# Half of an input projection by seven-product block multiplication for six of seven feature chunks, and a head without the early spatial-weight transpose

## The chip, the cores and the metric

One core of a Trainium2 chip. The metric is the device time of one execution in microseconds (us), a median over runs. A profiled span is about 1.7 us shorter than the time of the run that it was taken from (231.8 and 233.52 for the kernel before), so spans are compared with spans and timed runs with timed runs.

In the views of the profile PE is the tensor engine and PEld its weight loads, DVE is the vector engine, ACT the scalar engine, POOL the Pool engine, and SPq the queue that issues most transfers. A row of a timeline has the start and length in us, then engine, line of the kernel, operation, what it writes<-reads, its shape, how many in a row, and in brackets the idle time before it with what ended it. PSUM ("psum") is the memory that products are summed in; a bank here is a piece of it of 128x512 fp32.

## The reference

Two blocks with residuals on a sequence of 2048 tokens of width 512, in bf16: linear attention with 32 heads, then a gated MLP whose gate mixes tokens through a 2048x2048 spatial weight.

```python
h  = x + A(layernorm(x), wqkv, wo)              # linear attention
def B(x, w_in, w_sp, b_sp, w_out):              # on layernorm(h)
    z  = gelu(x @ w_in)                         # 2048 x 1792, F/2 = 896
    z1 = z[..., :896]                           # first half: the change is here
    z2 = layernorm(z[..., 896:])
    g  = einsum('ts,bsf->btf', w_sp, z2) + b_sp
    return (z1 * g) @ w_out
h2 = h + B(layernorm(h), ...)
```

## The kernel before

The program is a list of operations with data dependences; a fixed order string says in what order each engine takes its own, and semaphore waits follow from the dependences. So moving an operation within an engine's order is an edit of that string. The parts that the change touches:

```python
def matmuls(out_ap, pairs, start=True, stop=True, onto=False):   # L402: one matmul per pair
    ...
# first half of the input projection, transposed: 7 feature chunks x 4 token groups of 512
Z1B = [6, 7]
k = 0
for tg in range(NG):
    for fc in range(KF):
        b = Z1B[k % 2]
        k += 1
        matmuls(bank(b), [(win1[:, c, fc * P:(fc + 1) * P], hnT[:, c, tg * GW:(tg + 1) * GW]) for c in range(KD)])
        act(z1T[:, fc, tg * GW:(tg + 1) * GW], bank(b), ACT.Gelu_apprx_tanh, GW).soft.add(table.i)
# (cut) the spatial weight comes by transposing DMA, 16 row tiles; the first EARLY = 1 of them whole and in the head
for i, t in enumerate(order):
    w = NT // 2 if EARLY <= i < NT // 2 else NT
    for j in range(0, NT, w):
        op = dma_t(wsp[:, j:j + w, t * P:(t + 1) * P], B_w_sp[t * P:(t + 1) * P, j * P:(j + w) * P], ...)
        ...
        if i < EARLY:
            first_xt.soft.add(op.i)     # the head's own transposes queue behind it
```

In the head (the first 20 us) tiles of x are normalised, transposed (six by the tensor engine, ten by DMA), multiplied by the key weight, and summed with their keys. The second half of the projection ("z2") starts at about 65 us, and the spatial product with its own seven-product cells at about 120.

Of the kernel before, what the change touches and what calls it, by code (L numbers as in the profile page):

```python
# [18 lines left out]
class _Op:
# [233 lines left out]
def bass_sequential_preLN__linear_attn_block__mixer_gmlp__prompt_kernel(  # L253
# [130 lines left out]
    def bank(b, n=512, lo=0):  # L384
        return psum[:, b, lo:lo + n]
# [220 lines left out]
    def next_pair():  # L606
        pc[0] += 1
        return PAIRS[pc[0] % 2]

    CB, first_xt, second = [4, 5, 6, 7], None, None  # L610
    HEAD, SINGLE = 6, 4
    ACTS = (1,)
    QSPLIT, KSPLIT, CACT = (6, 7), (), 2


    def k_unit(n):
        nonlocal first_xt, second
        b = next_pair()
        for i in (n, n + 1):
            if i in ACTS:  # L620
                s = st[0][:, i, :]
                act(sh_t[0], x[:, i, :], ACT.Identity, D, accum=s[:, 0:1])
                act(sh_t[1], x[:, i, :], ACT.Square, D, scale=D ** -0.5, accum=s[:, 1:2])
                moments(s, 6, D)
                rpow(s[:, 7:8], rs[0][:, i, 0:1])
            else:
                op = stats(x, 0, i)
                if i == 0:
                    second = warmup(16, 60, op)
                if n == 0:  # L630
                    rstd_act(st[0], rs[0], i, 1, 6)
        if n == 2:
            rstd_act(st[0], rs[0], n, 2, 6)
        elif n:
            rstd(st[0], rs[0], n, 2, 6, n >= HEAD)
        for i in (n, n + 1):
            norm("DVE" if n < HEAD else "ACT", xn[:, i, :], x[:, i, :], st[0], rs[0], i, 6, D)
            if n < HEAD:
                pe_transposes(xn[:, i, :], b + i % 2, xnT, i, second)
            else:  # L640
                g.last = dma_t(xnT[:, :, i * P:(i + 1) * P], xn[:, i, :], f"xt{i}")
                if i == HEAD:
                    first_xt = g.last
        for i in (n, n + 1):
            matmuls(bank(b + i % 2), [(xnT[:, c, i * P:(i + 1) * P], wqkv[:, c, D:2 * D]) for c in range(KD)])
        if n < SINGLE:
            for i in (n, n + 1):
                phi(pk[:, i:i + 1, :], b + i % 2, 1)
        else:
            phi(pk[:, n:n + 2, :], b, 2, n in KSPLIT)  # L650

        def fn(pe, i):
            inst = None
            for c in range(KD):
                inst = pe.matmul(bank(CB[c]), lhsT=xn[:, i, c * P:(c + 1) * P], rhs=pk[:, i, :],  # L655
                                 start=i == 0, stop=i == NT - 1)
# [180 lines left out]
    order = [t for p in range(NG // 2) for tg in (p, p + NG // 2) for t in range(tg * TPG, (tg + 1) * TPG)]
    prev = late
# [181 lines left out]
```

## Time and profile before

| | before |
|---|---|
| median of the timed runs | 233.21 us |
| profiled span | 231.8 us |
| tensor engine with work | 224.6 us, 97% |
| first pair "pk,xn" of tiles 4 and 5 starts | 20.32 us |
| first z2 group starts | 65.01 us |
| last matmul starts | 228.95 us |

The last three rows are marks read off the timeline: the start of one easily recognised instruction at the end of the head, at the start of the second part, and at the end. Because the tensor engine is nearly always full, the difference of a mark between two kernels says in which of three stretches time was won or lost. The page's lines stand in the prediction.

### The profile page before, as it was taken

What the parts mean: (1) busy time and instruction counts of PE and PEld (TensorE: products, weight loads), DVE (VectorE), ACT (ScalarE), POOL (GpSimd) and SP (SyncE); (2) the same over time, 40 slices, a digit from 0 to 9 for tenths busy, and PEclk for the clock granted to TensorE, in tenths of its full rate; (3) what the DMA queues carried; (4) which work ended last, traced back from release to release, by engine and by line L of the source; (5) the groups of instructions that cost most, each with busy time, mean ns of one, the idle gap of its engine ahead of it and who ended that gap; (6) DMA issues with size and microseconds to landing.
All of it is one profiled execution on the core that took longest, in us unless ns stands there. A gap on an engine that the chain in (4) does not pass through costs nothing.

```text
span 231.8 us, 3231 instructions
## 1 busy us (share of the span) xinstructions
PE 224.6 (97%) x1180; PEld 112.1 (48%) x1203; DVE 161.6 (70%) x323; ACT 104.3 (45%) x193; POOL 44.2 (19%) x134
## 2 busy tenths in 40 slices
PE   8997999999999999999999999999999999999995
PEld 8543444453445443454544444444455555555452
DVE  4998755646987550237489989979795566785485
ACT  5694754399989876679862010101021211123010
POOL 3436300000466608023771000000000000000000
PEclk9999999999999999999999999999999999999999
DMA  5893259947546635968999700000000000020025
GB/s 182 263 214 70 59 138 230 315 147 181 114 89 136 117 71 121 183 126 188 185 228 197 159 3 0 0 0 0 3 0 1 0 3 0 20 72 3 0 80 191
DMA packets 58864, 23.68 MB, mean 102 GB/s; under 512 B 48480, under 2 KB 58720, under 8 KB 58848
## 3 DMA queue, kind: packets, MB, share of 16 engines
q1 hardware_dynamic: 58144, 22.88, 44.7%
q10 hardware_dynamic: 704, 0.59, 0.8%
q8 instruction: 9, 0.15, 0.3%
q14 instruction: 7, 0.06, 0.1%
HBM read 7.47 MB, written 2.10 MB: 41 GB/s over the span
## 4 chain that ended last, share of the span: by engine, by line
PE 86%; DMA 6%; ACT 3%; DVE 2%; issue 1%; SPq 0%
PE psum L402 70%; PE psum L802 6%; PE psum L655 5%; PE psum L805 4%; DMA x<-in_A_x_dram 3%; DMA xnT<-xn 2%; DMA hnT<-hn 1%; DVE st L511 1%; ACT sh L421 1%; ACT xn L421 1%; ACT e L421 0%; ACT xnT L421 0%; PE psum L751 0%; PE psum L676 0%; PE psum L720 0%
## 5 line engine op out<-in xcount | busy, mean ns | idle before, releaser
L421 ACT ACTIVATE psum<-psum 128x256 f32<-128x256 f32 (+1 forms) x33 | 14.3, 445 | 90.8 <-PE psum L402 63.1
L402 PE MATMUL psum<-wsp,z 128*128 128x512 bf16 x204 | 47.5, 379 | 0.2
L402 PEld LDWEIGHTS psum<-wsp,z 128*128 128x128 bf16 x208 | 20.4, 98 | 22.9
L402 PE MATMUL psum<-hnT,win 128*128 128x512 bf16 x108 | 25.6, 379 | 0.2
L421 ACT ACTIVATE e<-psum 128x1024 bf16<-128x1024 f32 (+1 forms) x18 | 16.7, 926 | 15.2 <-PE psum L402 14.3
L402 PE MATMUL psum<-t,s 128*128 128x512 bf16 x94 | 22.1, 379 | 0.1
L421 ACT ACTIVATE z1T<-psum 128x512 bf16<-128x512 f32 x28 | 16.6, 594 | 4.9 <-PE psum L402 4.8
L802 PE MATMUL psum<-win,hnT 128*128 128x512 bf16 x64 | 16.4, 379 | 0.4 <-DMA hnT<-hn 0.4
L402 PE MATMUL psum<-wout,z1T 128*128 128x256 bf16 (+1 forms) x82 | 16.6, 314 | 0.1
L402 PEld LDWEIGHTS psum<-hnT,win 128*128 128x128 bf16 x112 | 10.0, 98 | 13.2 <-ACT z1T L421 3.8
L402 PE MATMUL psum<-wqkv,xnT 128*128 128x512 bf16 x61 | 14.8, 380 | 1.4 <-DMA xnT<-xn 1.2
L421 ACT ACTIVATE z<-psum 128x896 bf16<-128x896 f32 x16 | 14.5, 909 | 2.9 <-PE psum L805 2.8
L402 PE MATMUL psum<-xnT,wqkv 128*128 128x512 bf16 x61 | 15.1, 379 | 0.3 <-issue 0.2
L655 PE MATMUL psum<-pk,xn 128*128 128x512 bf16 x64 | 15.3, 379 | 0.0
L402 PE MATMUL psum<-m,pqT 128*128 128x512 bf16 x62 | 14.7, 379 | 0.3 <-DVE h L776 0.2
L776 DVE SCALAR_TENSOR_TENSOR h<-psum,x 128x512 bf16<-128x512 f32 x16 | 10.8, 688 | 5.2 <-PE psum L402 5.1
L402 PEld LDWEIGHTS psum<-t,s 128*128 128x128 bf16 x96 | 9.4, 98 | 10.3
L582 DVE TENSOR_SCALAR e<-e 128x1024 bf16<-128x1024 bf16 (+1 forms) x18 | 7.1, 397 | 9.1 <-ACT e L421 9.0
L805 PE MATMUL psum<-win,hnT 128*128 128x384 bf16 x64 | 13.0, 326 | 0.0
L924 DVE TENSOR_TENSOR u<-psum,bsp 128x512 bf16<-128x512 f32 x16 | 11.0, 687 | 2.8 <-PE psum L402 2.7
L556 DVE TENSOR_SCALAR z<-z,st,rs 128x896 bf16<-128x896 bf16 x16 | 7.2, 493 | 7.3 <-POOL rs L519 7.3
L511 DVE BATCH_NORM_STATS2 st<-x 128x6 f32<-128x512 bf16 x15 | 9.7, 677 | 3.6 <-DMA x<-in_A_x_dram 3.6
(113 smaller groups left out, 349.3 us busy)
## 6 DMA issues: line engine op xcount, KB each, us to landing
r<-rcp SPq DMA_DIRECT2D x16, 128.0 KB, 2.6
out_dram<-h SPq DMA_DIRECT2D x15, 128.0 KB, 1.8
win<-in_B_w_in_dram SPq DMA_DIRECT2D x2, 896.0 KB, 6.6
x<-in_A_x_dram SPq DMA_DIRECT2D x6, 256.0 KB, 4.5
wqkv<-in_A_wqkv_dram SPq DMA_DIRECT2D x2, 512.0 KB, 5.2
wout<-in_B_w_out_dram SPq DMA_DIRECT2D x1, 896.0 KB, 7.2
wo<-in_A_wo_dram SPq DMA_DIRECT2D x1, 512.0 KB, 8.3
bsp<-in_B_b_sp_dram SPq DMA_DIRECT2D x1, 512.0 KB, 5.1
```

The costliest lines, as they stand in the source:

```text
L402: inst = pe.matmul(out_ap, lhsT=a, rhs=b, start=start and i == 0, stop=stop and i == len(pairs) - 1, **kw)
L421: return g.add("ACT", lambda ac: ac.activation(out_ap, in_ap, func, **kw), [in_ap, *extra], [out_ap] + ([accum] if accum is not None else []),
L511: dve(lambda v: v.bn_stats(s[:, 0:6], src[:, n, :]), [src[:, n, :]], [s[:, 0:6]], D)
L556: return dve(lambda v: v.tensor_scalar(dst, src, mean, rst, op0=ALU.subtract, op1=ALU.mult), [src, mean, rst], [dst], w + 460, acc=4)
L582: dve(lambda v: v.tensor_scalar(e, e, 1.0, EPS_PHI, op0=ALU.min, op1=ALU.add), [e], [e], w * GW, acc=4)
L655: inst = pe.matmul(bank(CB[c]), lhsT=xn[:, i, c * P:(c + 1) * P], rhs=pk[:, i, :], start=i == 0, stop=i == NT - 1)
L776: dve(lambda v, n=n, b=b, s=s: v.scalar_tensor_tensor(h[:, n, :], bank(b), 1.0, x[:, n, :], op0=ALU.mult, op1=ALU.add, accum_out=s[:, 0:1] ...
L802: pe.matmul(bank(b), lhsT=hnT[:, c, n * P:(n + 1) * P], rhs=win2[:, c, 0:GW], start=c == 0, stop=c == KD - 1)
L805: inst = pe.matmul(bank(b + 1, F2), lhsT=hnT[:, c, n * P:(n + 1) * P], rhs=win2[:, c, GW:FH], start=c == 0, stop=c == KD - 1)
L924: dve(lambda v: v.tensor_tensor(t, bank(b), add, ALU.add), [bank(b), add], [t], GW, ps=True)
```

## The change

Its intent: with feature chunks k and k + 3, even and odd token tiles, and the 512-long sum split in two, four output blocks make one cell. The ordinary way takes 4 groups x 4 matmuls = 16; seven block products of 2 matmuls take 14, at the price of sums of weights, of inputs and of products. Six cells replace 24 of the 28 groups; the seventh chunk stays ordinary. The sums of inputs and weights lie in columns of the spatial weight's buffer that are loaded later (token groups 1 and 3). The early load of that weight goes too. The head's first loads, statistics and the whole order string are changed with it.

```diff
-EARLY = 1
+EARLY = 0
-ORDER = "c-jTQ17H..."                       (cut)
+ORDER = "c-jrogMt..."                       (cut)
...
+    def strassen(k, q, banks, p5):
+        A, B, C, E = banks
...
+        matmuls(quad(A), list(zip(w11, a11)))
+        copy(bank(B), bank(A))
+        matmuls(quad(E), list(zip(t1, s1)))
+        copy(p5, bank(E))
+        matmuls(quad(A), list(zip(w21, a12)), **onto)
+        gelu(k, q, 0, A)
+        matmuls(quad(B), list(zip(t2, s2)), **onto)
+        dve(lambda v: v.tensor_tensor(bank(C), bank(B), p5, ALU.add), [bank(B), p5], [bank(C)], GW, ps=True)
+        matmuls(quad(B), list(zip(t3, s3)), **onto)
+        matmuls(quad(C), list(zip(w22, s4)), **onto)
+        gelu(k + HF, q, 0, C)
+        dve(lambda v: v.tensor_tensor(bank(E), bank(B), p5, ALU.add), [bank(B), p5], [bank(E)], GW, ps=True)
+        matmuls(quad(B), list(zip(t4, a22)), **onto)
+        gelu(k + HF, q, 1, E)
+        gelu(k, q, 1, B)
...
+    comb(ts[0], w12, w11, ALU.subtract)      # 4 weight sums; the same for 4 input sums in each half
...
+        for k in range(HF):
+            if k not in CLASSIC.get(2 * q, ()):
+                strassen(k, q, ZB[cells % len(ZB)], p5z[cells % 2])
```

Here w and a are blocks of the weights and the inputs, t and s their sums, and A, B, C, E the four PSUM banks of a cell.

More of the change, by code (lines that the diff above doesn't have):

```diff
@@ L13 @@
 GRAN = 16
-EARLY = 1
+EARLY = 0
 SEM_NS = 45.0
-ORDER = "c-jTQ17HvU00h8Cwq47%ZQHhO+qGrewr$(CZ5wwH5gAbt9Wf9Su@D<^5Eu2800D@ED2Rr5$b~$}jl4*LqyUHz2nE3iiC_qhWJrz_NQp#9j8w>n{3w9JNQ(-ngvO|hifD@XNQl%(gMui6bjW~0NROh(gp4SL;;4eE$c!dvhAgOttSEtOsEO>Tj&A6I?kI_#D23)|fpBPrmgt4v=!-tcfm*16wy2FdXpPdSi+UJ`GAN7sXn-*oi}6^7B{+=bSc-PYiE=294rqh+XoyA_fPol{e&~-u=!i}@g3dUILzsYxn1sn#foYh6Ay|pf2#+ubi&cn#)i{b{IDz9BieU)ENCaUNMq>@uVLGOw3%X(^W?%v4<1|iU78YVH*5eGG;uKz@fg0)sp5qy2V-AL61U6tJ7GW`VU^_NpGqzwZ=3x)^VkdTCH_qWK_F+E`U@Nxa3a;WjF5n_A;U+HQ8gAh_Zr~N(;5FXjHtypN?&2OEA~+u)1Vi#2BJdF+G7{h8F`nQjKHvvF;uk*QAHLu-zTqprBPPMH49!ps!&o$9Gb*DoGNUja<1-H9G91J6H)1dqQ!@`UGdlA!3-hx8(=aX5F+DRdBQvoaOS2ZqeEfr~EJ*P$$}kwSF*|cGCkwGWb1{GkSeQjvl*L$=3Au#z*pj)~gSA<lCE13Fn3xr~m}Oa?OIe4l*qXiBmVH=}l~|co*p6$smJQgDjaZfK*^@Qcm`&J=eVLTWS%RgQgvq#t$(4dlnUc-9hbgp-TbWvEG@MgdjoUbaBiWA~*pZ#sp99#L138Gxxt%+>f-5<d={22=)L1pSjx(4+d%2HY*p1EDg4LN)sgzl1704hC<zRMaR}SM4Hc=L(Q$~$qCQai^o?%vHQ+DN0PUTiE<y9W#S3VU`K^0aZ713E9VR02z2^CXml~fs(S1Fa%9UkQ|-sKg(;Z>H?6TW2y&EkF@;6bkE25#hNj^S92<4*44A&%#4&f#3H;yg~^ah~9OF63cO;wEn9J>KU7KIBQB;yb?Q2cF}3Uf@OU=4r0xHD2c>HdQk<R|~aND^2DCPUIq1RAp7tA3o(X{$&+a)fawcHHBAeB~u%<RXep;2X#~@bygR3RRn!waD`A!g;Xtl<a6HOO+MlazT_>w;wS!NL|x`<J|+}NRAhbU5B}sY-e!CyP!xqyXh~rdRbgcXD4~8ckrFG3s;h>gD~3KZreZ0!!YP`PDvshRnBr-G`e?9ftFC6Kj%I3zhN_+hs;_2ixVmYIrfQJ7tG{|^l~!w-rYle*HCMybQzO(*qclz%G+MnBr16@ddFrkC8lzd7sC8PPC0eMpO5(Aaqyw6xrCOuOTBh~dsLfiWE!wJs+NPvltP@(U?b@Xk+N71*p}jh+L)xvK+Nb?GqCGmQ<4Wk0I;GP(qeMQY#LnfjI;RvquM4`QD@y5$itl8;rcb)A54x<Yx}&?grJK5^+`g{|O6>#=@JBt;L#6U#J<|(4(Nm@MXT8=drE_{e*B8CiS7q=!z125;*AFFk7XQ*uW%O_T6a7bjmEXZ^!*XbcabAaX2#0lehjSWda#m+{HWzR~M{q<(avn!@WJh-t7jkw-a|{=DKF4t^$8-+obP*SIF_&>!7k3HQbA88kBR6&vH*hmIbxD_ULr-!GH+OlrbSw9A8~1h}w{}IBb|qK#1o!hq_jP{{a67kkdk^#=5AiTp@nBbVIoEInS95jObS>9*M|bu{*Ku8UcMnhTR8MmUZ}Mgj^(+r}Cy(?DPxlsg@np|*kViPsvpvsqJl6}n$V)um3%%G&J<g-u)nmQfqrA+kywYpD*6SSG!F@yV+|!}F)$jF2x7E#KyxJ=~-s`==+q~U7ywkh<AMVe{ZU"
@@ new lines @@
+ORDER = "c-jrogMttU00qE@tj)G<d$VoZwz=81ZQHhO+jiZ}FHA&4MpVQ_03sm@q9HnBASPlVHsT;Y5+E1yAUE;?AdJumgRlsO;0S?m2#=5uk{}V1A{mk+1yUju5+fh-BNYmu5YnPNDxw0Kpb{D(9uguo(x4y;BONlJ2+|`EnUE1hQ4Cp88C8%OjnNcYP!-uw1KCj=-BAKv(F5I364j6c)zJ*i(Go4t6TQ#}z0n3WQ46h53bj!Obx|5+Fb3mL5A`t?<FO1&upDjC8aYuG<<K7O&>sWP7yZxy4bTvSFc3@85uI=t2XO?4FaZ-W8I!OAE3q0=Fb#vT4na7IV~BuNIDz9Bg5el}kywLK7>%izj?U<U8JLOrSb&o_jagWT^;nBDIE5E@iOG73DVnP1c!t@SgP|CP4cLf9Sd2~Bf$f-!dDx6C*o!^biGA3G-8hG{*otj9kNr4+E4YelxPaukh!jexRJx8ExP+Uyj9Yk%*LZ_hxQ#owi~G2T2MErG2*HqihX{Ox07m3{JjN4*W>|({DE`DJe83NU#AkfLH^kt-|GR(TJHFx%Vlo!PGaP>-G9xi6qi~wyG7e)i9#b(IQ!_L3Fh8>}I`c9O$*eRBFdqvtEz>bQGcY5?zX--mEXA^{$%M?t?99QOEX`a@z;cYwKo(+Q7GY7=VKLTXU6$YyCSqciXBpP!V%B2|wq^xZWF=N+71n11He@3<W^N{7awcVQCS!NDWG}8^8&+ixR%Z(KW;3Q_6Sm?~F5_CZWlwJ5R+eOHZDShs;ZP3a6pr9jj^uRC;Bby&HP&ELHfMTeP&>9~U+!UMrBzn#Wfo;uPMu*oWm5-sWIuLdS7uUwX4G~L;AoEFSPo<^1u?hssWS(09LIA9cXB4DaTaHDIp=UL=kYAh@jTaY0w?hT^XLe3sDJ{MSA~>cg;iWdRZvBAhwHh4CA5(jSxP0<jnmbIGc<$~IiLGjM!UG1`+0yzSxm=xmz7jnl~qnxc$}Mfj|+K_D|mt{d6I*<fQvYpr+A4oHA}NKM{|`-^E6)zv`~vwR^@e-Z&*QZSy4}TjaBrN&sbH}^oRHPjt^K}?^#0+d7Xb*Tc=r9{|G(j3*O)(zT{0d)nhi+WxnET-r{E7CiQ_e^@Yt<OJDhobrfFTxrz}KponUsAN<LW{Kfiepcbm9;0mFTil_K$rr$io!%U#n3?<3>#Lx<(u!^SWilKyxsYFVwBx<NeYOS_vshw)2U23CtilktQtoHiMSW2o+imfP$qi~9<xZ0?#I<L;^pdRX~ZtAED>aL#ZqCM)PUh1oU8mMjRuT8q7!RoC68ls^Zra>C6AdS)p?bB&J)M%a2SdGzmZP5;$)plLc1dY@<P0~88)_QH$8g0;8?bjn+)NUQrL><*$9nxhT&@mm?RUOuK9nn*r&~2U5HGS7f-O(vM(Oo^$3%%AGJr{gKFZDw=^;oZTPm8rgOSMePwL&YkN^kW}A9YK$d|warUVrsdAM{0E^+})gOW*Wce^kY^9L#n~|5H5&cL;ZIeTQ@?hjBQEc0&g^g2OtzQ#+EYx|$<9s-ro&J359_Ii{<-iPN~YV>_1PxRc{Mq2s!<<2i{FyM_}uk<&VzlRKHyJEJqWsq470Gdq(TIE$M(tFt?&v$>UPI*)U^ky|^5bGe`cozHEY--TSnh270{-POfh)XiPoJzUCVT*4*Y$E97?E!@)O+{JBO(cN9%ecjHL+|TXZ)6+f3z1-WAJ;hT!%`-gHgFVZ$-QNQ|$8$Zz^SsdWy};|e!Hd1fOT5ur9pvF2=*>Rv6CUAB9_lUL=3yS`?cV7Ze(6yj>m45Lah~Au9^;9g<Xzt5WnSUkUgNbs<&!?`Gd}BA-sipE@1?%z<v!r^KIhk7<&{3_BR=GVzTn5c<jcO|Cw}Uye&%bw;ak4r>%QsRe&`3j=evIEcYf~=PT>Ns?1;|mbx!IEj^Z~y=EHvO)qdpr{^<VzBaZh("
@@ L478, in first_load @@
         op.bias = 1e6
-        if q:
+        if q and q[-1] is not behind:
             op.soft.add(q[-1].i)
@@ L487, in load_x @@
         return first_load(eng, x[:, n:n + w, :], x_d[n * P:(n + w) * P, :], f"x{n}", lat, behind)
-    x0 = load_x("SP", 0, 1, 2150)
-    load_x("ACT", 1, 1, 2250)
-    x2 = load_x("SP", 2, 1, 2500)
-    load_x("ACT", 3, 1, 2500)
-    wk = [first_load(eng, wqkv[:, c:c + 2, D:2 * D], A_wqkv[c * P:(c + 2) * P, D:2 * D], f"wk{c}", 3500)
-          for eng, c in (("SP", 0), ("ACT", 2))]
-    for n, lat, behind in ((4, 2000, x2), (6, 2200, x2), (8, 1900, wk[0]), (10, 2100, wk[0]), (12, 2300, wk[0]),
-                           (14, 2500, wk[0])):
+    load_x("SP", 0, 1, 2150)
+    load_x("ACT", 1, 1, 2300)
+    x2 = load_x("SP", 2, 1, 2300)
+    load_x("ACT", 3, 1, 2550)
+    first_load("SP", wqkv[:, 0:2, D:2 * D], A_wqkv[0:2 * P, D:2 * D], "wka", 4200)
+    wk = first_load("ACT", wqkv[:, 2:4, D:2 * D], A_wqkv[2 * P:4 * P, D:2 * D], "wkb", 4400)
+    for n, lat, behind in ((4, 3000, x2), (6, 3200, x2), (8, 3850, wk), (10, 4000, wk), (12, 4200, wk), (14, 4400, wk)):
         load_x("SP", n, 2, lat, behind)
-    first_load("SP", wqkv[:, :, 0:D], A_wqkv[:, 0:D], "wq", 3400)
+    first_load("SP", wqkv[:, :, 0:D], A_wqkv[:, 0:D], "wq", 3500)
     exp_table = g.add("ACT", lambda ac: ac.preload_act_table_set("natural_log_exp_and_others"), [], [], cost=1300)
@@ L611, in bass_sequential_preLN__linear_attn_block__mixer_gmlp__prompt_kernel @@
     HEAD, SINGLE = 6, 4
-    ACTS = (1,)
+    ACTS, ND, LEAD, lead = (1,), (), 0, []
     QSPLIT, KSPLIT, CACT = (6, 7), (), 2
@@ L618, in k_unit @@
         b = next_pair()
+        first = len(g.ops)
         for i in (n, n + 1):
@@ L631, in k_unit @@
                     rstd_act(st[0], rs[0], i, 1, 6)
+        if n == 2 and LEAD:
+            for op in g.ops[first:]:
+                if op.eng == "DVE":
+                    op.soft.add(lead[LEAD - 1].i)
         if n == 2:
@@ L634, in k_unit @@
         elif n:
-            rstd(st[0], rs[0], n, 2, 6, n >= HEAD)
+            rstd(st[0], rs[0], n, 2, 6, n >= HEAD or n in ND or n + 1 in ND)
         for i in (n, n + 1):
-            norm("DVE" if n < HEAD else "ACT", xn[:, i, :], x[:, i, :], st[0], rs[0], i, 6, D)
+            lead.append(norm("DVE" if n < HEAD and i not in ND else "ACT", xn[:, i, :], x[:, i, :], st[0], rs[0], i, 6, D))
             if n < HEAD:
@@ L647, in k_unit @@
             for i in (n, n + 1):
-                phi(pk[:, i:i + 1, :], b + i % 2, 1)
+                phi(pk[:, i:i + 1, :], b + i % 2, 1, i in KSPLIT)
         else:
@@ L767, in bass_sequential_preLN__linear_attn_block__mixer_gmlp__prompt_kernel @@
     AB, HPAIR = [4, 5, 7], 2
+    CLASSIC, ZB = {}, [(4, 5, 6, 7), (7, 4, 5, 6)]
     def HN(n):
@@ L825, in bass_sequential_preLN__linear_attn_block__mixer_gmlp__prompt_kernel, with gelu @@
     dma("SP", bsp, B_b_sp.partition_broadcast(P), "bsp", issue=1500, lat=2500).deps.add(g.last.i)
-    Z1B = [6, 7]
-    k = 0
-    for tg in range(NG):
-        for fc in range(KF):
-            b = Z1B[k % 2]
-            k += 1
-            matmuls(bank(b), [(win1[:, c, fc * P:(fc + 1) * P], hnT[:, c, tg * GW:(tg + 1) * GW]) for c in range(KD)])
-            act(z1T[:, fc, tg * GW:(tg + 1) * GW], bank(b), ACT.Gelu_apprx_tanh, GW).soft.add(table.i)
+    def gelu(fc, q, odd, b):
+        o = z1T[:, fc, :].rearrange("p (g two t) -> p g two t", two=2, t=P)[:, 4 * q:4 * q + 4, odd, :]
+        act(o, quad(b), ACT.Gelu_apprx_tanh, GW).soft.add(table.i)
@@ new lines, in classic @@
+    def classic(fc, tg, b):
+        matmuls(bank(b), [(win1[:, c, fc * P:(fc + 1) * P], hnT[:, c, tg * GW:(tg + 1) * GW]) for c in range(KD)])
+        act(z1T[:, fc, tg * GW:(tg + 1) * GW], bank(b), ACT.Gelu_apprx_tanh, GW).soft.add(table.i)
+    def strassen(k, q, banks, p5):
+        A, B, C, E = banks
+        fl, fh = slice(k * P, (k + 1) * P), slice((k + HF) * P, (k + HF + 1) * P)
+        w11, w12, w21, w22 = ([win1[:, 2 * i + c, f] for c in (0, 1)] for i in (0, 1) for f in (fl, fh))
+        a11, a12, _, a22 = ([hx[:, 2 * i + c, 4 * q:4 * q + 4, odd, :] for c in (0, 1)] for odd in (0, 1) for i in (0, 1))
+        t1, t2, t3, t4 = ([t[:, c, fl] for c in (0, 1)] for t in zt)
+        s1, s2, s3, s4 = ([s[:, c, :].rearrange("p (g t) -> p g t", t=P) for c in (0, 1)] for s in zs[q])
+        onto = dict(start=False, onto=True)
+        matmuls(quad(A), list(zip(w11, a11)))
[13 more added lines that the diff above has]
+        gelu(k, q, 1, B)
@@ new lines, in bass_sequential_preLN__linear_attn_block__mixer_gmlp__prompt_kernel, with comb @@
+    quad = lambda b: bank(b).rearrange("p (g t) -> p g t", t=P)
+    copy = lambda o, i: act(o, i, ACT.Copy, GW)
+    hx = hnT.rearrange("p c (g two t) -> p c g two t", two=2, t=P)
+    prow = lambda r, tg: wsp[:, r:r + 2, tg * GW:(tg + 1) * GW]
+    zt = [prow(2 * i, 3) for i in range(4)]
+    zs = [[prow(8 * q + 2 * i, 1) for i in range(4)] for q in (0, 1)]
+    p5z = [g.sbuf(f"p5z{b}", o_r + b * GW * 4, [GW], FP32) for b in (0, 1)]
+    def comb(out_ap, a, b, op):
+        n = 2 * out_ap.shape[2]
+        if len(a.shape) == 4:
+            out_ap, a, b = (v if len(v.shape) == 4 else v.rearrange("p c (g t) -> p c g t", t=P) for v in (out_ap, a, b))
+        dve(lambda v: v.tensor_tensor(out_ap, a, b, op), [a, b], [out_ap], n, acc=2)
@@ new lines, in bass_sequential_preLN__linear_attn_block__mixer_gmlp__prompt_kernel @@
+    w11, w12, w21, w22 = (win1[:, 2 * i:2 * i + 2, f:f + HF * P] for i in (0, 1) for f in (0, HF * P))
+    ts = [t[:, :, 0:HF * P] for t in zt]
+    comb(ts[0], w12, w11, ALU.subtract)
+    comb(ts[1], w22, ts[0], ALU.subtract)
+    comb(ts[2], w22, w12, ALU.subtract)
+    comb(ts[3], w21, ts[1], ALU.subtract)
+    cells = 0
+    for q in (0, 1):
+        a11, a12, a21, a22 = (hx[:, 2 * i:2 * i + 2, 4 * q:4 * q + 4, odd, :] for odd in (0, 1) for i in (0, 1))
+        for tg in (2 * q, 2 * q + 1):
+            classic(KF - 1, tg, 6)
+            for fc in CLASSIC.get(tg, ()):
+                classic(fc, tg, 6)
+        s1, s2, s3, s4 = zs[q]
+        comb(s1, a21, a22, ALU.add)
+        comb(s2, s1, a11, ALU.subtract)
+        comb(s3, a11, a21, ALU.subtract)
+        comb(s4, a12, s2, ALU.subtract)
+        for k in range(HF):
+            if k not in CLASSIC.get(2 * q, ()):
+                strassen(k, q, ZB[cells % len(ZB)], p5z[cells % 2])
+                cells += 1
```

## The prediction

> **What bounds the kernel now.** I read the page's totals and slices first, then the chain that ended last, then the stretches of ten microseconds, the timeline of the head, and last the groups by shape.
>
> ```profile
> PE 224.6 (97%) x1180; PEld 112.1 (48%) x1203; DVE 161.6 (70%) x323; ACT 104.3 (45%) x193; POOL 44.2 (19%) x134
> PE 86%; DMA 6%; ACT 3%; DVE 2%; issue 1%; SPq 0%
> ```
>
> The totals and the chain agree: the tensor engine has work in 97% of the span and carries 86% of the chain. In the 40 slices its granted clock is full throughout. So time changes by (a) the number of tensor-engine columns and (b) the few places where it waits. It is idle 231.8 - 224.6 = 7.2 us. The stretches say where:
>
> ```profile
> 0.00:10.00 10.00, 8.84 (x76) 7.45 (x78) 6.04 (x16) 6.45 (x15) 2.79 (x19) 1.00 0.68 212
> 10.00:20.00 10.00, 8.69 (x45) 3.67 (x45) 9.90 (x26) 6.32 (x10) 4.67 (x13) 1.00 0.93 196
> ...
> 50.00:60.00 10.00, 9.53 (x60) 4.50 (x60) 6.76 (x13) 9.61 (x16) 0.46 (x2) 1.00 0.46 107
> 60.00:70.00 10.00, 9.34 (x47) 3.96 (x46) 9.09 (x25) 8.46 (x18) 5.71 (x16) 1.00 0.60 119
> ...
> 110.00:120.00 10.00, 9.95 (x52) 5.04 (x52) 6.17 (x16) 8.38 (x16) 7.75 (x22) 1.00 1.18 201
> 120.00:130.00 10.00, 9.95 (x47) 4.50 (x46) 9.90 (x14) 1.92 (x4) 1.79 (x4) 1.00 1.13 212
> ```
>
> After start and stretch come tensor matmul, weight load, vector, scalar, Pool, granted clock, DMA share and GB/s. 1.2 us is lost before 10 us, 1.3 us in 10 to 20, 1.1 us in 50 to 70, about 2.8 us at the end (the last sums and stores); elsewhere 0.05 us in ten. So the input projection, which lies between 73 and 120, is bound by the tensor engine alone, with the scalar engine at 70 to 96% beside it. The head's timeline:
>
> ```profile
> 8.86 5.56 SPq L435 DMA_TRANSPOSE wsp<-in_B_w_sp_dram  x1
> 13.59 0.81 ACT L421 ACTIVATE xn<-x,rs 128x512 bf16<-128x512 bf16 x1
> 14.47 16.78 SPq L435 DMA_TRANSPOSE xnT<-xn  x9
> 14.63 2.75 PE L655 MATMUL psum<-pk,xn 128*128 128x512 bf16 x12
> 16.61 1.22 DVE L587 SCALAR_TENSOR_TENSOR pk<-psum,e 128x1024 bf16<-128x1024 f32 x1
> 18.58 1.90 PE L402 MATMUL psum<-wqkv,xnT 128*128 128x512 bf16 x7 [1.20 <-DMA xnT<-xn]
> ```
>
> One early transpose of the spatial weight holds the queue from 8.86 to 14.42. The first normalised tile that must be transposed by DMA is ready at 13.21 (its activation starts at 12.41 and takes 0.80), but its transpose is issued only at 14.47, and the tensor engine, whose other work ends at 17.38, stands still until 18.58.
>
> ```profile
> L402 PE MATMUL psum<-hnT,win 128*128 128x512 bf16 x108 | 25.6, 379 | 0.2
> L421 ACT ACTIVATE z1T<-psum 128x512 bf16<-128x512 f32 x28 | 16.6, 594 | 4.9 <-PE psum L402 4.8
> L421 ACT ACTIVATE psum<-psum 128x512 f32<-128x512 f32 x12 | 7.0, 581 | 42.8 <-PE psum L402 23.7 <-DVE u L924 19.0
> L924 DVE TENSOR_TENSOR u<-psum,p 128x512 bf16<-128x512 f32 x12 | 8.2, 688 | 0.9 <-PE psum L402 0.6
> L929 DVE TENSOR_TENSOR s<-z 128x1024 bf16<-128x1024 bf16 x3 | 2.1, 686 | 0.0
> L929 DVE TENSOR_TENSOR wsp<-z1T 128x768 bf16<-128x768 bf16 x4 | 2.2, 551 | 0.0
> ```
>
> The first two rows are the projection that the change touches (28 x 4 = 112 matmuls in the program, 4 records missing). The other four are the prices for what it adds: the kernel already has such copies and sums in its later block multiplications.
>
> **What the Trainium skill says.** "TensorE: Matmul & The Clock Gate", Back-to-back issue gap, gives N/2.4 + 2.5 ns for a matmul behind another, 216 ns at N = 512, and calls 131 ns sustained in real kernels. The trace sides with 216: four matmuls of this shape run in 0.86 us on the chain. The 379 ns of the rows is a pipelined duration and must not be multiplied. "ScalarE: Activation LUTs", What ACT_TABLE_LOAD costs, says back-to-back activations overlap by about 93 ns; here a z1T activation of 0.60 us at 76.46 is followed at 76.95, so each costs 0.49 us of the engine. "VectorE: DVE Perf Modes", the perf-mode tier table, puts tensor_tensor at double rate on bf16 in SBUF and single rate with PSUM; the rows agree (1024 bf16 elements in 686 ns, 512 from PSUM in 688). "DMA: Bandwidth & Descriptors", Issuing engines are not separate DMA queues, says all DMAs share the same 16 engines and interleave; in agreement, that first transpose landed 4.06 us after issue, beside the spatial weight's traffic, where the kernel's median is 2.5.
>
> **The change part by part.**
> Tensor engine: 28 groups of 4 matmuls become 4 ordinary groups (16) and 6 cells of seven products with 2 matmuls each (84). 112 - 100 = 12 fewer, at 0.216 us: **-2.6 us**. In this stretch it is the bound, so it counts in full unless a wait replaces it. The operand of 4 blocks of 128 columns keeps 512 columns, so I keep 216 ns.
> Scalar engine: the same 28 GELUs, plus 2 copies a cell: 12 x 0.58 = 7.0 us busy, some 5.8 us of occupancy.
> Vector engine: 2 PSUM sums a cell, 12 x 0.69 = 8.3 us, 4 weight sums x 0.55 = 2.2 us and 8 token sums x 0.69 = 5.5 us: +16 us, to about 178.
> None of these lies on the path by itself, if the order keeps them ahead. The new order string, decoded, puts the weight sums near 43 us, where the vector engine has room, interleaves cells 1 to 3 with the second-half projection (z2), and carries cells 4 to 6 into the first spatial products. Up to the last z2 group there remain 60 of the matmuls where there were 104; so z2 ends about 9.5 us earlier and the rest comes after. Occupancy from the first z2 group (65.0) to its end: tensor engine 64 x 0.38 (z2) + 60 x 0.216 + 8 x 0.86 (attention output) = 44 us; scalar engine 13.5 (z2) + 6.5 (squares) + 5.6 (statistics of h) + 1.3 (table) + 22 x 0.49 (GELUs and copies) = 37.7 us, 86%. By hand through two cells, each copy or sum ends 0.1 to 1 us before its reader. I put new waits at 0.5 us.
> Head: the early transpose goes. The first transpose can issue at about 13.3, land at the median 2.5 us later, near 16, and the second (ready 14.40) near 17. The matmul pair can start when its predecessors end, about 17.0, and then the next pair waits for the vector engine's sum over tiles 4 and 5: in the new order two statistics come ahead of it, so it ends near 18.7 instead of 17.83. The next pair started at 20.32 to 20.48; it would start at about 18.8: **-1.6 us**. After it the tensor engine is full to 48, so the gain survives there.
> Given back: the removed half megabyte must come later. Ahead of the output weight (wo) the queue now holds three half transposes of the spatial weight instead of two (6.47 us for two in the timeline), so wo, which lands at 49.8 and is used at 52.2, lands near 51.2 and is wanted at 50.6: **+0.4 us** with some luck.
> Sum: -2.6 - 1.6 + 0.5 + 0.4 = -3.3 us, 229.9.
>
> **Rivals.**
> 1. The scalar engine becomes the bound of z2: 86% on average, but 93% in the last eight groups (15.3 of 16.4 us). For it: copies stand between products of one cell, which has only four banks. Against: it stood at 84 to 96% in 70 to 80 and 100 to 120 with the tensor engine at 9.95 of 10. It would give back 1 to 2.5 us: 231 to 232.
> 2. The head gives nothing: the vector engine is at 9.90 in 10 to 20, so its sums may replace the DMA as the wait, or the gain vanishes at 50 to 60, where the scalar engine is at 9.61 and wo comes late. Then only the matmuls remain: about 231.
> 3. The spatial weight comes late. Its columns for groups 1 and 3 hold the cells' operands, so their 8 transposes start only when the last cells are read, about 126 instead of 108; at 2.7 us each they end near 150, wanted near 154. Margin some 4 us; late, it would cost its lateness, against the saving, and 233 is possible.
> 4. Both gains come whole and the new order also closes part of the 1.1 us at 50 to 70: 228.5.
>
> **Range and chances.** The matmul saving is arithmetic and sure to about 0.2 us; the head is good for 0.5 to 1.9; waits take 0.2 to 2. That gives 228.7 to 231.6. Faster by over 2% needs less than 228.5, more than all my terms without a loss: 10%. Slower by over 2% needs 4.7 us on top of a lost saving, only by rival 3 in a bad form: 2%.
>
> **What would show it.** Right: about 100 matmuls less missing records in the projection's groups; no queue entry for the spatial weight before 30 us; the idle of 1.20 us before the matmul near 18.58 gone, with the pair after it near 18.8; tensor-engine idle in 66 to 130 still near 0.05 in ten. Wrong: waits of the tensor engine for the psum copies, the PSUM sums or z1T in that stretch (rival 1); for wo or m near 51 (rival 2); the first matmuls of the second spatial half waiting for the spatial weight near 155 (rival 3). A spacing other than 216 ns in the cells would break the main term.

## The result, and the profile after

The changed kernel took 230.76 us (230.63 to 230.90), the kernel before 233.21 beside it: ratio 0.9891, 95% interval 0.9876 to 0.9905, which is inside the range. (Ratios are the mean time of one kernel's fast runs over that of the other's of the same rounds, so not quite the ratio of the medians quoted.) Two later repeats gave 0.9885 and 0.9869.

The page of the changed kernel, totals and chain:

```profile
PE 221.9 (97%) x1168; PEld 110.0 (48%) x1191; DVE 174.5 (76%) x347; ACT 109.6 (48%) x205; POOL 47.7 (21%) x134
...
PE 91%; DVE 2%; issue 2%; POOL 1%; DMA 1%; ACT 1%
```

These are 12 matmul records fewer (1180 to 1168; some records are missing in both, and complete traces of the two programs have 1203 and 1191) and 12.9 us more vector work, where the prediction had 16; DMA's share of the chain fell from 6% to 1%. The stretches, same columns as in the prediction:

```profile
10.00:20.00 10.00, 9.95 (x52) 4.46 (x52) 9.75 (x25) 7.18 (x12) 4.33 (x12) 1.00 0.52 138
50.00:60.00 10.00, 9.85 (x56) 4.34 (x55) 7.58 (x15) 9.78 (x17) 1.36 (x4) 1.00 0.69 154
60.00:70.00 10.00, 9.18 (x46) 3.76 (x44) 9.54 (x28) 8.14 (x19) 6.99 (x17) 1.00 0.54 118
110.00:120.00 10.00, 9.59 (x45) 4.11 (x45) 8.90 (x17) 4.83 (x10) 2.93 (x7) 1.00 0.43 52
```

The hole of the tensor engine at 10 to 20 us closed (8.69 to 9.95). A new one of 0.4 us opened at 110 to 120. The timeline of the head of the changed kernel:

```profile
13.59 9.59 SPq L435 DMA_TRANSPOSE xnT<-xn  x5
...
14.98 2.75 PE L659 MATMUL psum<-pk,xn 128*128 128x512 bf16 x12
...
17.57 1.89 PE L402 MATMUL psum<-wqkv,xnT 128*128 128x512 bf16 x7
...
19.30 1.89 PE L659 MATMUL psum<-pk,xn 128*128 128x512 bf16 x8
```

No spatial weight ahead of the transposes, no idle ahead of the pair at 17.57 (14.98 + 12 x 0.216 = 17.57), none ahead of 19.30 (17.57 + 8 x 0.216). The groups of the projection, with what was added:

```profile
L402 PE MATMUL psum<-hnT,win 128*128 128x512 bf16 x39 | 10.7, 379 | 0.1
...
L402 PE MATMUL psum<-wsp 128*128 128x512 bf16 x35 | 10.0, 379 | 0.4 <-DVE psum L856 0.4
...
L860 DVE TENSOR_TENSOR psum<-psum,p5z 128x512 f32<-128x512 f32 x6 | 4.2, 698 | 3.2 <-PE psum L402 3.2
L856 DVE TENSOR_TENSOR psum<-psum,p5z 128x512 f32<-128x512 f32 x6 | 4.2, 694 | 1.8 <-PE psum L402 1.7
...
L421 ACT ACTIVATE p5z<-psum 128x512 f32<-128x512 f32 x6 | 3.6, 607 | 0.7 <-PE psum L402 0.7
```

The matmuls of one cell go by their operands: "hnT,win" (plain inputs and weights), "wsp" (sums of both), and mixed ones (two more rows of 12 and 11). The one row with idle time names its releaser, the PSUM sum of L856. Where it happens, timeline of the changed kernel:

```profile
117.06 0.59 PE L402 MATMUL psum<-wsp 128*128 128x512 bf16 x2
...
117.50 0.59 PE L402 MATMUL psum<-hnT,win 128*128 128x512 bf16 x2
117.69 0.70 DVE L856 TENSOR_TENSOR psum<-psum,p5z 128x512 f32<-128x512 f32 x1 [0.21 <-PE psum L402]
...
118.45 0.60 PE L402 MATMUL psum<-wsp 128*128 128x512 bf16 x2 [0.36 <-DVE psum L856]
```

This is the fifth cell. The pair "t2,s2" at 117.06 fills bank B; the sum reads it from 117.69 to 118.39; the pair "t3,s3" may only then add onto it. One pair (0.43 us) lies between. Measured between the starts of matmuls, the step into 118.45 is 0.741 us where 0.216 would follow, so 0.525 us is lost; the 0.36 in the brackets is less because a matmul's end is modelled.

Where the time came from, by the three marks (us):

| stretch | before | after | difference |
|---|---|---|---|
| to the end of the head | 20.32 | 19.30 | -1.02 |
| head to first z2 group | 44.69 | 44.70 | 0.0 |
| first z2 group to last matmul | 163.94 | 162.32 | -1.62 |
| span after the last matmul | 2.84 | 2.85 | 0.0 |

### The profile page after: what moved, and what is told of

It is laid out like the page before. It is cut to its first block, busy times and chain, and to the rows that moved or that the text cites. A ratio compares the mean times of both kernels' runs of the same rounds, so it can differ in the third digit from the quotient of the medians.

```text
span 229.2 us, 3241 instructions
## 1 busy us (share of the span) xinstructions
PE 221.9 (97%) x1168; PEld 110.0 (48%) x1191; DVE 174.5 (76%) x347; ACT 109.6 (48%) x205; POOL 47.7 (21%) x134
## 4 chain that ended last, share of the span: by engine, by line
PE 91%; DVE 2%; issue 2%; POOL 1%; DMA 1%; ACT 1%
PE psum L402 72%; PE psum L807 6%; PE psum L659 6%; PE psum L810 5%; DMA x<-in_A_x_dram 1%; ACT sh L421 1%; DVE h L981 1%; DVE h L781 1%; POOL rs L550 1%; ACT m L421 0%; PE psum L755 0%; POOL st L534 0%; PE psum L680 0%; PE psum L569 0%; PE psum L724 0%
## 5 line engine op out<-in xcount | busy, mean ns | idle before, releaser
L421 ACT ACTIVATE psum<-psum 128x256 f32<-128x256 f32 (+1 forms) x39 | 17.7, 467 | 83.6 <-PE psum L402 57.0
L421 ACT ACTIVATE z1T<-psum 128x512 bf16<-128x512 f32 x28 | 16.1, 601 | 8.1 <-PE psum L402 5.5
L402 PE MATMUL psum<-wsp 128*128 128x256 bf16 (+1 forms) x89 | 19.3, 315 | 0.4 <-DVE psum L856 0.4
L989 DVE TENSOR_TENSOR u<-psum,p 128x512 bf16<-128x512 f32 x12 | 8.3, 688 | 8.1 <-PE psum L402 8.0
L534 POOL TENSOR_SCALAR st<-st 128x1 f32<-128x1 f32 x10 | 3.9, 391 | 40.0 <-ACT sh L421 32.2
L402 PEld LDWEIGHTS psum<-wsp 128*128 128x128 bf16 x90 | 8.2, 98 | 8.2 <-DVE psum L856 1.0
```

The lines of the kernel that those rows point to most:

```text
L402: inst = pe.matmul(out_ap, lhsT=a, rhs=b, start=start and i == 0, stop=stop and i == len(pairs) - 1, **kw)
L421: return g.add("ACT", lambda ac: ac.activation(out_ap, in_ap, func, **kw), [in_ap, *extra], [out_ap] + ([accum] if accum is not None else []),
L534: pool(lambda p: p.tensor_scalar(s[:, 2:3], s[:, 0:1], s[:, 0:1], -1.0 / (n * n), op0=ALU.mult, op1=ALU.mult), [s[:, 0:1]], [s[:, 2:3]], 240)
L989: dve(lambda v: v.tensor_tensor(t, bank(b), add, ALU.add), [bank(b), add], [t], GW, ps=True)
```

## The experiments

Twelve runs, two of them the changed kernel again, in three batches of five rounds, each beside 11 executions of the kernel before (medians 233.86, 233.52, 233.80). The third batch (experiments 9 to 12) ran on another chip than the first two; ratios are always within a batch. My theory: three terms act separately, head -1.0 to -1.6, matmuls -2.6, new waits of the cells about +1. Rivals: the head's gain is luck, or is lost further on; the scalar or the vector engine bounds the cells.

**1. The changed kernel again.** No edit. Its first statistics start at 3.83 us in the first profile against 3.36 in the kernel before; was a late first load hiding part of the head's gain?

> The changed kernel once more, unaltered, for a second profile. Question: in the first profile the first tile's statistics start at 3.83 us, 0.47 later than in the kernel before, and the first full matmuls at 8.53 instead of 7.90. Theory (chance of the first load): here the statistics start at another time than 3.83 by over 0.15 us, and the matmuls move by as much. Rival (made by the new order): 3.83 within 0.1 again. Time in both: 230.8, ratio 0.989.

230.79 us, ratio 0.9885 (0.9862 to 0.9908). The first statistics started at 3.26, 0.57 earlier, and the end of the head stood at 19.28 against 19.30. The theory had the matmuls move with the statistics; they moved by 0.02. So a late first load did not take the missing 0.6 us.

**2. The head alone.** The changed kernel's head and order up to the first z2 group, then the projection and order of before.

```diff
 # on the changed kernel
-    def strassen(...): ...   cells, sums
+    Z1B = [6, 7] ...         the 28 ordinary groups
-ORDER = (changed)
+ORDER = (changed, up to the first z2 group) + (before, from there)
```

> The head and the order of the changed kernel up to the first z2 group, then the ordinary projection of 112 matmuls in the order of before; no early transpose of the spatial weight. Theory: the head's gain is separate and kept to the end: 1.0 us, some 232.2, ratio 0.9957. Rival (it vanishes at 50 to 60, where the scalar engine binds, or in the tail): 233.0 or more, ratio over 0.999. My recorded prediction would want 1.2 us after the late output weight.

233.38 us, ratio 0.9989 (0.9969 to 1.0009): no gain, a miss. The head ended at 19.40 and z2 started at 64.12, 0.9 ahead of before; then the tensor engine waited at the seam. My splice had put two attention-output tiles in one order on the tensor engine and in the other on the vector engine. Timeline of this kernel, tensor engine:

```profile
65.64 1.04 PE L402 MATMUL psum<-m,pqT 128*128 128x512 bf16 x4
67.28 1.90 PE L402 MATMUL psum<-m,pqT 128*128 128x512 bf16 x8 [0.60 <-DVE h L781]
```

A step of 0.764 us lost, a product of my edit. So it was repeated.

**3. The head alone, seam mended.**

```diff
-ORDER = ... 375, 363 ...      (tensor engine: tile 9's product behind tile 10's)
+ORDER = ... 363, 375 ...      (exchanged, to fit the vector engine)
```

> head_only with its splice mended. There the head led by 0.9 us up to the first z2 group and lost it at 66 us, where the tensor engine took the attention outputs of tiles 10 and 9 in that order while the vector engine freed their banks in the other. Here the two groups are swapped to fit. Theory (the head's gain is real and that loss was my splice): 0.6 us less than head_only, 232.7, 0.9960 of before, and the lead of 0.9 at the first z2 group still there at the last one. Rival (the gain is lost after 60 us in any order): 233.4 again.

232.78 us, ratio 0.9973 (0.9958 to 0.9988). The long wait at the seam is gone: one run of matmuls from 65.25, with a step of 0.16 us lost in it at 66.28, which the changed kernel has too.

```profile
65.25 3.79 PE L402 MATMUL psum<-m,pqT 128*128 128x512 bf16 x16
```

z2 starts 1.28 us ahead of the kernel before and the last matmul 1.11 ahead. The head's gain is real and is kept to the end. The timed runs show less of it, 0.6 us (0.3 to 1.0); the profile is of the fastest of the five.

**4. The projection alone.** The head of before with its early call; cells, sums and late loads of the change.

```diff
 # on the kernel before (EARLY = 1 kept)
-    Z1B = [6, 7] ...         the 28 ordinary groups
+    def strassen(...): ...   cells, sums
+ORDER: weight sums ahead of 49 us, the changed order from the first z2 group on
```

> The head of before, with its early transpose, then the seven-product cells in the order of the changed kernel; the four weight sums moved behind the z sums, near 49 us, because the weight arrives later there. Theory: 2.6 us of matmuls less 0.7 us of new waits: 1.6 to 1.9 us less, 231.4, ratio 0.9925. Rival (the parts need each other: the later start of the transposes or the moved sums cost): over 232.0, ratio over 0.995.

232.49 us, ratio 0.9954 (0.9933 to 0.9976). The same kind of seam wait cost 0.857 us at 66.7. Mended in the next.

**5. The projection alone, seam mended.**

```diff
-ORDER = ... 326, 346, 349 ...
+ORDER = ... 346, 349, 326 ...    (vector engine: two residual sums earlier)
```

> proj_only with its splice mended: the residual sums of tiles 6 and 7 go ahead of the norm of tile 2 on the vector engine, as in the kernel before, where a wait of 0.69 us arose at 67 us. Theory: that wait goes, 0.7 us less than proj_only, 231.8, ratio 0.992, so cells alone are worth some 1.6 us. Rival (the cells need the head's earlier times): 232.4 again.

232.09 us, ratio 0.9941 (0.9920 to 0.9962), somewhat short of the expected 0.992. The seam wait is gone. The outputs are right. From the first z2 group to the last matmul 162.62 us against 163.94 before. That is 1.3 of the 1.6 that the whole change wins there. In this profile the head ended at 21.05, in that of experiment 4 at 19.82, in the kernel before at 20.32: with the early call the head's end varies by over a microsecond.

**6. Filler moved into the wait.** A spatial product of 8 matmuls, which stood behind the fifth cell's pair "t3,s3", goes ahead of it.

```diff
-ORDER = ... 636, 634, 638, 639, 723, 645 ...
+ORDER = ... 636, 634, 723, 638, 639, 645 ...
```

> The changed kernel with one spatial product of eight matmuls moved ahead of the third product pair of the fifth cell, where the tensor engine stands 0.36 us for a PSUM sum. Theory (that wait is a hole in the order: 0.43 us of work between two products that a 0.70 us sum links): the wait goes, 0.3 us less than after_again, ratio 0.9878. Rival (the vector engine is the bound there, the wait moves to a later product): the same as after_again within 0.1 us.

232.13 us, ratio 0.9941 (0.9919 to 0.9963), 1.3 us slower than the changed kernel beside it, which neither theory nor rival had expected. The wait near 118 is gone, and two larger ones stand behind it, in the tensor engine's timeline of this kernel:

```profile
119.90 0.59 PE L402 MATMUL psum<-wsp,win 128*128 128x512 bf16 x2
121.49 0.60 PE L402 MATMUL psum<-hnT,win 128*128 128x512 bf16 x2 [0.99 <-ACT z1T L421]
122.47 0.60 PE L402 MATMUL psum<-wsp 128*128 128x512 bf16 x2 [0.37 <-ACT z1T L421]
```

The sixth cell's first product needs the bank that the fifth cell's GELU must first read, and that GELU comes behind "t3,s3", then a PSUM sum, then its own 0.6 us. The filler had been covering this longer chain. The steps lose 1.16 and 0.54 us for the 0.53 won: +1.2, and the stretch from z2 to the last matmul is 163.57 against 162.40.

**7. Six added activations,** to measure the scalar engine's slack in z2.

```diff
+    for _ in range(6):
+        act(u_t[0], h[:, 0, :], ACT.Copy, GW)      # result unread; in the trace at 79 to 105 us
```

> The changed kernel with six more activations of 128x512 from SBUF to an unused buffer, one behind six of the z2 activations, 6 x 0.53 = 3.2 us of the scalar engine between 78 and 107. My recorded count left it 14% idle there, 6 us. Theory (slack): at most 0.4 us more than the changed kernel, 230.8 to 231.2. Rival 1 of the record (the scalar engine binds z2): 2.5 to 3.2 us more, 233.5.

232.43 us, ratio 0.9962 (0.9947 to 0.9977). From z2 to the last matmul 163.98 against 162.32 to 162.40: 1.6 us came through of 3.8 us busy time added (6 x 0.63). This lies between the theory (at most 0.4) and the rival (2.5 to 3.2). New waits of 0.2 to 0.45 us stand before products of the changed projection and one z2 product, two of them in the tensor engine's timeline:

```profile
80.35 0.60 PE L402 MATMUL psum<-hnT,win 128*128 128x512 bf16 x2 [0.29 <-ACT psum L421]
...
101.23 0.61 PE L402 MATMUL psum<-hnT,win 128*128 128x512 bf16 x2 [0.29 <-ACT z1T L421]
```

The changed kernel has one lost step that ends with the scalar engine (0.18 us before the z2 product at 70.8), so the scalar engine doesn't bound it, but it has little left.

**8. Five cells.** The sixth cell back to four ordinary groups.

```diff
-                strassen(k, q, ZB[cells % len(ZB)], p5z[cells % 2])
+                if cells == 5:
+                    for fc, tg, b in ((2, 2, 7), (2, 3, 6), (5, 2, 4), (5, 3, 5)):
+                        classic(fc, tg, b)
+                else:
+                    strassen(k, q, ZB[cells % len(ZB)], p5z[cells % 2])
```

> The changed kernel with its sixth cell (14 matmuls, 2 copies, 2 sums) taken back to four ordinary groups (16 matmuls). Theory A (each cell is worth its 2 x 0.216 = 0.43 us, the wait of 0.36 to 0.52 us near 118 belongs to the fifth cell and stays): 0.4 us more, 231.2. Theory B (the wait is the price of two cells in a row with too little other work between them, and goes with the sixth): the same within 0.15 us, 230.8.

233.21 us, ratio 0.9995 (0.9981 to 1.0010), as neither theory had expected. The loss of 0.53 near 118 stays, so it belongs to the fifth cell and not to the sixth behind it. The rest of the result is confounded by my edit: in fitting the order string I put the last ordinary group ahead of some sums "s" of the vector engine. Those sums overwrite memory of the weight that this group still reads, so now they had to wait for it. Timeline of this kernel, vector engine:

```profile
126.60 1.29 DVE L998 TENSOR_TENSOR s<-z 128x1024 bf16<-128x1024 bf16 x2 [4.28 <-PE psum L402]
```

The tensor engine then waited some 2 us for those sums at 128.5. What one cell is worth by itself, this run does not say.

**9. The changed kernel a third time,** as the yardstick of the last batch; no edit.

> The changed kernel unaltered, as the yardstick of this batch. Expected 230.4 to 231.1 us, ratio to the kernel before 0.986 to 0.991, with the step of about 0.74 us (0.53 lost) near 118 us between the third product pair of the fifth cell and the pair before it. If that step were absent here, it would be chance and not part of the order.

230.66 us, ratio 0.9869 (0.9846 to 0.9892). The step near 118 loses 0.526 again; the head ends at 18.74.

**10. The filler split,** two matmuls of it into the wait and six behind.

```diff
-        matmuls(bank(A), [(z2[:, HT + s, fl], wsp[:, HT + s, lo]) for s in ss], start=False, onto=True)
+        for part in ((range(2), range(2, HT)) if cnt[1] == 2 else (ss,)):
+            matmuls(bank(A), [(z2[:, HT + s, fl], wsp[:, HT + s, lo]) for s in part], start=False, onto=True)
-ORDER = ... 634, 638, 639, 723, 645 ...
+ORDER = ... 634, 723, 638, 639, 724, 645 ...
```

> The changed kernel with the first two of the eight matmuls of the spatial product that stands behind the fifth cell's third pair moved ahead of that pair; six stay behind it. Theory: the pair waits for the vector engine's PSUM sum, 0.53 us, so two matmuls (0.43 us) fit into the wait, and the six left (1.30 us) still cover the chain of sum and GELU that frees the bank of the sixth cell (it ended some 0.6 us before its reader). Expected: loss near 118 at 0.1 us or less, nothing new at 120 to 122, the first t,s product of the spatial part 0.4 us earlier against the first z2 group, 230.3 to 230.5 us, 0.4 below the yardstick. Rival: the wait only moves, as when all eight were moved (232.1): then a new step of 0.4 us or more shows near 120.5 and the time is that of the yardstick or worse.

230.95 us, ratio 0.9882 (0.9857 to 0.9907): no gain on the yardstick. As expected the loss near 118 fell, to 0.094 us, and the sixth cell's first product follows without a wait. But its second product now waits. Timeline, tensor engine:

```profile
120.60 0.59 PE L402 MATMUL psum<-hnT,win 128*128 128x512 bf16 x2
121.44 0.61 PE L402 MATMUL psum<-wsp 128*128 128x512 bf16 x2 [0.24 <-ACT z1T L421]
```

It loses 0.407 us. I had checked the first product's bank and not the second's: its bank is freed by the third GELU of a run of three (119.81 to 121.38), at the head of which stands one that waits until 119.81 for a PSUM sum. From z2 to the last matmul 162.40, as without the edit. The rival of this run was right. A reorder of those three GELUs might free the bank earlier; it was not tried.

**11. Only the early call taken out** of the kernel before.

```diff
-EARLY = 1
+EARLY = 0
 # instruction order of before; the load's two halves go to the other late ones
```

> The kernel before with only the early transposed load of the spatial weight taken out; its two halves go where the other late ones go. Instruction order of all engines otherwise that of before. Theory: the call alone held the queue until 14.4 us and made the head 1.1 us later on average, so this kernel is 0.8 to 1.3 us faster than before (232.3 to 232.8, ratio 0.995 to 0.997) and the first pk,xn pair of tiles 4 and 5 stands at 19.0 to 19.6 us instead of 20.3. Rival: the reordered statistics, norms and first loads of the change do it; then the pair stays at 20.0 or later or another wait takes its place, and the time is within 0.3 us of before.

232.26 us, ratio 0.9938 (0.9915 to 0.9960), a little better than expected. Timeline of its head:

```profile
13.27 9.27 SPq L435 DMA_TRANSPOSE xnT<-xn  x5
...
14.66 2.75 PE L655 MATMUL psum<-pk,xn 128*128 128x512 bf16 x12
...
17.25 1.89 PE L402 MATMUL psum<-wqkv,xnT 128*128 128x512 bf16 x8
18.98 1.89 PE L655 MATMUL psum<-pk,xn 128*128 128x512 bf16 x8
```

The pair stands at 18.98 instead of 20.32, 1.34 us earlier, and the last matmul is 1.34 earlier (227.61 against 228.95). The first transpose of xn is issued at 13.27 instead of 14.47, and its landing takes 3.18 us instead of 4.06. A measure that leaves out when the first loads came is the time from the start of the 12 matmuls ahead to the start of the pair. It is 4.32 us in all eleven profiles without the call, just 20 matmuls at 0.216, and 5.69, 5.28 and 5.86 in the three with it. So the call alone, worth 1.0 to 1.5 us, is the whole of the head's gain. The changed first loads and statistics add nothing that shows: with them the pair stood at 18.74 to 19.40 in ten profiles. By timed runs this kernel even gained more (1.4 us, 0.9 to 2.0) than the whole changed head in experiment 3 (0.6, 0.3 to 1.0), in another batch and on another chip; the intervals just meet, and whether the rest of the changed head costs something is open.

**12. Eight added vector sums,** the counterpart of experiment 7.

```diff
+    for _ in range(8):
+        dve(lambda v: v.tensor_tensor(u_t[1], h[:, 1, :], h[:, 2, :], ALU.add), ...)   # unread; in the trace at 84 to 102 us
```

> The changed kernel with eight added vector sums of 128x512 bf16 in SBUF, some 0.42 us each, 3.4 us in all, spread over the stretch of the second-half projection and the cells, 66 to 126 us; nobody reads the result. Theory: the vector engine has slack there although it is busy 89 to 95 per cent of its slices, the scalar engine being the nearer limit; then less than a third of the added work comes through, 230.7 to 231.8. Rival: the vector engine is as near to binding as the scalar engine, where 3.2 us of added work cost 1.65; then 232.2 or more.

231.90 us, ratio 0.9915 (0.9894 to 0.9937), just above the expected range; part of that is the head, which ended 0.3 later than in the yardstick. From z2 to the last matmul 163.09 against 162.40: 0.7 us of 3.2 us busy time (8 x 0.405) came through. It did so in one place, where a PSUM sum of a cell was pushed back (the timeline's line of the pair that waits for it):

```profile
88.87 0.61 PE L402 MATMUL psum<-wsp,win 128*128 128x512 bf16 x2 [0.60 <-DVE psum L858]
```

So in these two placings the vector engine has somewhat more slack than the scalar engine, and what costs is not its load but the moment of those sums.

## Why the prediction was right, by its own steps

| step of the prediction | predicted | measured | from |
|---|---|---|---|
| 12 fewer matmuls | -2.6 | -2.6 | 12 records fewer, spacing 0.216 us kept |
| head | -1.6 | -1.0 to -1.3 | this pair of profiles -1.02; experiment 11 -1.34 |
| new waits | +0.5 | +1.0, of it 0.6 in cells | steps of matmul starts after the first z2 group |
| output weight late | +0.4 | 0.0 | head to first z2 group 44.69 and 44.70 |
| sum | -3.3 | -2.6 to -3.1 | spans 229.17, 229.23 and 228.68 against 231.79; timed medians -2.5, -3.1, -3.1 |

**Matmuls.** Right. Lost steps can be summed only in traces without missing records. After the first z2 group they sum to 0.01 us in experiment 11, whose order there is that of before, and to 1.07 in both repeats of the changed kernel (experiments 1 and 9). 2.59 - 1.06 = 1.53 of gain is to be expected in that stretch; these profiles show 1.53, the first profile 1.62.

**Head.** Right in cause, too large by 0.3 to 0.6 us. The mis-sized part is "the pair can start when its predecessors end, about 17.0" and "it would start at about 18.8", set against 20.32 to 20.48. Those predecessors are 12 matmuls that started at 14.63 in the kernel before; at 0.216 each they end issue at 17.22, and 8 more follow to 18.95. Against 20.32 the most to be had was 1.37, which experiment 11 nearly reaches. The wait for the vector engine's sum, which the prediction let set the new time, did not set it: the sum ended at 19.06, and the pair followed its predecessors without idle. In the changed kernel everything stood 0.35 later (14.98). Why was not settled: experiment 1 excludes the first load, and a third profile ended its head at 18.74, so it lies within what changes by chance.

**New waits.** Half as large as they turned out. "Each copy or sum ends 0.1 to 1 us before its reader" was worked by hand through two cells; the fifth cell alone loses 0.53 and a cell product at 88.4 another 0.08, so for the cells themselves 0.5 was nearly right. What the prediction left out stands elsewhere: 0.15 at 66.5, before an attention product that waits for a residual sum, and 0.18 at 70.8, before a z2 product that waits for the scalar engine. Experiment 3, which has no cells, loses the first of these too, so it comes with the new order.

**Output weight.** Wrong, harmlessly: it was issued at 41.07 and landed 6.7 us later, at 47.8, and its reader at 51.60 had no wait; I had estimated 51.2 for the landing. It was to land 1.4 us later than before and landed 2.0 earlier. It was issued 0.4 us earlier: three half transposes did stand ahead of it, but the transposes of xn were through at 30.33 instead of 33.13. And the landing took 6.7 us instead of 8.3; no run isolates why.

**The rivals.** The scalar engine (1) does not bound the changed kernel, but 1.6 us of 3.8 added came through, so the suspicion was near. The head's gain (2) is neither absent nor lost at 50 to 60 us: experiments 3 and 11. The spatial weight (3) came in time: its last transposes ended their issue at 145.6 and landed by 148.0, inside the margin that I had given, and no matmul of the second spatial half waits for them. Everything whole (4) is excluded by the 1.0 us of waits. Of the signs, two failed: the pair stood at 19.30 and not near 18.8, and the idle time in 110 to 120 was 0.41 in ten and not near 0.05. No version tried here is faster than the changed kernel.

## What to carry to other kernels

Here 12 fewer matmuls on a full tensor engine were worth their count times the spacing, minus the waits that the added copies, sums and the new order brought; look for such waits where an accumulating matmul must wait until another engine has read the same bank. Before moving filler into such a wait, follow every chain that the filler now covers, for each of the banks that the next cell will take: here two reorders moved the wait on, and one made it three times as large. A long transposing load placed early held back a short one on the critical path; taking it out alone was worth half of the whole change.

## What the Trainium skill lacked or had wrong

- "TensorE: Matmul & The Clock Gate", Back-to-back issue gap: it calls 131 ns sustained for N = 512 in real kernels. Nowhere in these runs is it seen: 12 matmuls from 14.98 to 17.57 us are 216 ns each, as are the cells' products on 4 blocks of 128 columns, and in all 14 traces no step from a full 128x128 matmul of 512 columns to the next is under 214 ns.
- "VectorE: DVE Perf Modes", the perf-mode tier table, has a column "any-PSUM" and does not say whether a PSUM destination counts; no page that I found times such a sum. A sum of a PSUM bank and an fp32 SBUF operand into another PSUM bank took 694 to 698 ns at 512 columns, hardly more than the 689 of one from PSUM into SBUF bf16.
- "DMA: Bandwidth & Descriptors", DMA Transpose (X-bar), states no time for which one transposing call occupies its issuing queue; elsewhere the page has a bandwidth for transposes, not this. One of 0.5 MB held it for 5.56 us, and taking that call out moved the head's end by 1.34 us; with it the head's end ranged from 19.82 to 21.05 us over three profiles, without it from 18.74 to 19.40 over eleven.
- No page that I found says how much of a cell's copies and sums on the other engines can hide; here 3.8 us of added scalar work cost 1.6 us and 3.2 us of added vector work 0.7 us.
